# Expert rows through a transposing DMA on ScalarE's queue, with cleared slots and an early read of the overflow count

## The chip, the cores and the metric

The kernel runs on one core of one Trainium2 chip. A core has five engines that run their own instruction queues: TensorE (PE in the profile, its weight loads PEld), VectorE (DVE), ScalarE (ACT), GpSimd (POOL) and SyncE (SP). Sixteen DMA engines move data between HBM and the core's SBUF for all queues. The metric is device time in microseconds of one execution; less is better.

## What is computed

An attention without softmax, then a mixture of experts in which each token goes to one expert.

```python
kv = np.einsum('bhsd,bhse->bhde', k, v)          # 8 batches, 8 heads, 576 tokens, 64 wide
out = np.einsum('bhsd,bhde->bhse', q, kv)
rms = np.sqrt(np.mean(out * out, axis=-1, keepdims=True) + 1e-06)
x = out / rms * g_norm                            # as rows: N = 4608, D = 512
logits = x @ w_gate                               # E = 8 experts
expert_idx = np.argmax(logits, axis=1)
probs = softmax(logits); gate_w = probs[range(N), expert_idx]
for e in range(E):
    mask = expert_idx == e
    ye = np.maximum(x[mask] @ w1[e], 0.0) @ w2[e] # F = 1024
    out[mask] = gate_w[mask, None] * ye
```

## The kernel before

**Attention.** The outer loop (line 789) runs over the batches, with one more round for the last tiles. For batch b it forms the 64x64 products of k and v (`kv_mm`), transposes q (`t_mm`), folds the product with an identity and with the gate's weights (`fold_mm`), and copies the results out of PSUM (`x_copy`). Mixed into that, the output tiles of the batch before are made: `o_mm` on TensorE, the square on ScalarE and its sum on VectorE (`o_red`), the root by Ln and Exp (`o_nrm`), and the scaled row as fp16 with the gate's partial sums (`o_x`). Two batches make a pair j with nine tiles of 128 tokens. SyncE loads k, v and q for batch b+2 while b is worked on; a half batch is five loads.

**Rows.** A row of `xrow` holds 512 fp16 values, the gate's weight (fp32) and the token's number (int32): 516 words of 16 bits, `ROW`, 1032 bytes. One `xrow` buffer holds three tiles; there are four of them. `g_norm` is not in the rows.

**Routing.** When a chunk of tiles is done, `route` (line 685) runs in steps between the tiles: the expert by a maximum on VectorE, ranks by matmuls with a triangular matrix (`rps`), the row's slot in `posi`, and then one indirect DMA for each tile, issued by GpSimd (line 743), that scatters 128 rows into the DRAM tensor `x_slots`, where expert e owns N rows from e·N. The chunks of pairs 0 and 1 are whole, pair 2 is cut in (0,3) and (3,9), pair 3 in three. `jobs` is a queue; `job()` runs one step of its first entry, twice in each tile.

**Groups.** Experts 0 to 2 first take the rows of the first 384 slots that have been filled when pair 2 has been routed (`early_rows`, `EARLY_TILES` = 3), and later their slots 384 to 639. Experts 3 to 7 take 640 slots (`SLOT_TILES` = 5) at once. So `groups` are three of K=3 tiles, three of K=2 and five of K=5. What doesn't fit in 640 slots goes by tiles of 128: one spill tile is always computed ahead of the last group, others in a loop at the end (`For_i`, line 854) whose count `n_more` is read into registers of all engines (line 850).

**A group.** `fetch` gathers its rows by one indirect DMA a tile on GpSimd (line 291) into one of three buffers `xl`; slots that hold no row are skipped by an index out of bounds, so `xl` is zeroed at the start (line 788). `xpose` turns a tile by four TensorE transposes into PSUM `xps` (line 325), and VectorE copies it out, times `g_norm`, into `xsT` (line 328). `stage1` makes the eight blocks `hp` of the hidden layer (line 345), and ScalarE writes the relu `hT` (line 353). `stage2` makes a tile of output `yp` (line 361), VectorE multiplies it by the gate's weight (line 366), and GpSimd scatters it to the output by the tokens' numbers (line 369). Next group's `xpose` stands between the tiles of `stage2`. Group n+2 is fetched in stage 1 of group n.

**Weights.** Every `w_step` casts one staged block of weights from fp32 to fp16 on VectorE (line 220) and lets SyncE load another block of 0.52 MB (lines 206, 210); four blocks are in flight. Eight blocks make an expert.

**What sets the order.** The kernel is written under a manual schedule: each engine executes its instructions in the order in which the Python code issues them, and a tile framework puts in the semaphore waits. `ffn` is a generator; `unit()` advances it by one step, in the last round of the attention twice a tile from its fourth tile on (line 832). The loop at the end and line 850 stand behind the manual part.

Of the kernel before, what the change touches and what calls it, by code (L numbers as in the profile page):

```python
# [11 lines left out]
F32 = mybir.dt.float32  # L12
# [33 lines left out]
def kernel(  # L46
# [109 lines left out]
    for j in range(4):  # L156
# [7 lines left out]
    xl_ring = [  # L164
        P_const.tile([128, SLOT_TILES, ROW], I16, tag=f"xl{n}", name=f"xl{n}") for n in range(3)
    ]
# [13 lines left out]
    def w_load(pool, bufs):  # L180
# [34 lines left out]
        w_staged.append((e, dst, st))  # L215

    def w_cast(engine):
        if w_staged:
            e, dst, st = w_staged.pop(0)
            engine.tensor_copy(dst, st)  # L220
            w_done[e] = w_done.get(e, 0) + 1
# [4 lines left out]
    def w_step():  # L226
# [11 lines left out]
    srow = P_const.tile([128, 8, SLOT_TILES], F32, tag="srow")  # L238
    nc.vector.tensor_tensor(
        srow, _bc(cv["srank"], 1, 8), _bc(cv["ebase"], 2, SLOT_TILES), op=ALU.add  # L240
    )

    def row_index(name, ctr, ne, nk):
        bad = P_const.tile([128, ne, nk], F32, tag="bad" + name, name="bad" + name)
        nc.vector.tensor_tensor(
            bad, _bc(cv["srank"][:, 0:nk], 1, ne), _bc(ctr[:, 0:ne], 2, nk), op=ALU.is_ge
        )
        idx = P_const.tile([128, ne, nk], I32, tag="idx" + name, name="idx" + name)
        nc.vector.scalar_tensor_tensor(
            out=idx, in0=bad, scalar=BIG, in1=srow[:, 0:ne, 0:nk], op0=ALU.mult, op1=ALU.add  # L250
        )
        badi = P_const.tile([128, ne, nk], I32, tag="badi" + name, name="badi" + name)
        nc.vector.tensor_scalar(badi, bad, BIG, None, op0=ALU.mult)
        return idx, badi
# [3 lines left out]
    def early_rows():  # L258
# [6 lines left out]
        for i in range(EARLY):  # L265
            groups[i].fetch()
# [6 lines left out]
    class Group:  # L273
        def __init__(self, n, e, k0, k1):
# [4 lines left out]
            self.xl = xl_ring[n % 3]  # L279
# [8 lines left out]
        def fetch(self):  # L288
            idx = rows[self.table][0]
            for k in range(self.K):  # L290
                nc.gpsimd.indirect_dma_start(  # L291
                    out=self.xl[:, k, :], out_offset=None, in_=xs.ap(),
                    in_offset=IndirectOffsetOnAxis(
                        ap=idx[:, self.e, self.k0 + k : self.k0 + k + 1], axis=0
                    ),
                    bounds_check=E * N - 1, oob_is_err=False,
                )

        def slot_ids(self):
            badi = rows[self.table][1]  # L300
# [3 lines left out]
                self.xl[:, 0 : self.K, D + 2 : D + 4].bitcast(I32),  # L304
                badi[:, self.e, self.k0 : self.k0 + self.K].unsqueeze(2), op=ALU.max,
            )

# [6 lines left out]
        def start(self):  # L314
            self.xsT = self.pool().tile(
                [128, 4, self.n], F16, tag="xsT" + self.tag(), bufs=1, name="xsT"
            )

        def tag(self):
            return ""  # L320

        def xpose(self, k):
            ps = PSA.tile([128, 4, 128], F16, tag="KV", bufs=2, name="xps")
            for c in range(4):
                nc.tensor.transpose(  # L325
                    ps[:, c, :], self.xl[:, k, c * 128 : (c + 1) * 128].bitcast(F16), ident16
                )
            nc.vector.tensor_scalar(  # L328
                self.xsT[:, :, k * 128 : (k + 1) * 128], ps, g2, None, op0=ALU.mult
            )  # L330

        def stage1(self, f):
            if f == 0:
                self.hT = self.pool().tile(
                    [128, 8, self.n], F16, tag="hT" + self.tag(), bufs=1, name="hT"
                )
# [18 lines left out]
        def stage2(self, k):  # L355
            if self.small:
                yp = PSA.tile([128, D], F32, tag="O", bufs=2, name="yp")
            else:
                yp = PSA.tile([128, D], F32, tag="T", bufs=2, name="yp")
            for f in range(8):  # L360
# [6 lines left out]
                y, yp, self.xl[:, k, D : D + 2].bitcast(F32), None, op0=ALU.mult  # L367
# [10 lines left out]
    class SpillGroup(Group):  # L378
        def __init__(self, tables, col, view):
            self.tables, self.col, self.view = tables, col, view  # L380
            self.e, self.K, self.n, self.step, self.small = "s", 1, 128, 128, False

        def tag(self):
            return "d"
# [25 lines left out]

    class LoopGroup(SpillGroup):
# [3 lines left out]
        def fetch(self):  # L415
            super().fetch()
            self.wd = (
# [73 lines left out]
    tabs = []  # L491
# [4 lines left out]
    def ffn():  # L496
        order = list(groups)
        cur = order[0]
        cur.start()
        for k in range(cur.K):  # L500
            cur.xpose(k)
            yield
        n = 0
        while n < len(order):
# [4 lines left out]
            for f in range(8):  # L509
# [3 lines left out]
                if f == 0 and 1 <= real and EARLY <= real + 2 < len(groups):  # L513
                    groups[real + 2].fetch()
# [4 lines left out]
                if f == 3 and cur.e == EARLY + 1:  # L519
                    spill = SpillGroup(tabs[0], slice(0, 1), out_views[E * SLOT_TILES])  # L520
                    spill.fetch()
                    order.insert(len(order) - 1, spill)
                yield
            nxt = order[n + 1] if n + 1 < len(order) else None
            todo = []
            if nxt is not None:
                nxt.start()
                todo = list(range(nxt.K))
                nxt.xpose(todo.pop(0))
            for k in range(cur.K):  # L530
# [3 lines left out]
                while todo and len(todo) > max(cur.K - 2 - k, 0):  # L534
                    nxt.xpose(todo.pop(0))
# [13 lines left out]
    with tc.tile_pool(name="pattn", bufs=1) as PA:  # L549
# [55 lines left out]
        def fold_mm(b):  # L605
            folds[b] = [
                PSA.tile([128, 4, 72], F32, tag="T", bufs=2, name=f"fold{b}{y}")
# [12 lines left out]
        def x_copy(b):  # L620
            kvx[b] = PA.tile([128, 2, 4, 72], F32, tag="kvx", bufs=3, name=f"kvx{b}")
            nc.scalar.copy(kvx[b][:, 0], folds[b][0])
            nc.vector.tensor_copy(kvx[b][:, 1], folds[b][1])
# [269 lines left out]
```

## Time and profile before

Three runs took 325.21, 326.92 and 331.18 us; the median is 326.92. The profiled execution took 330.94 us.

| What | Before |
|---|---|
| time of the profiled execution | 330.94 us |
| span from first to last instruction | 329.2 us |
| mean granted TensorE clock | 0.903 |
| busy TensorE, share of the span | 269.0 us, 82% |
| busy VectorE | 183.4 us, 56% |
| busy ScalarE | 119.9 us, 36% |
| busy GpSimd | 137.6 us, 42% |
| moved by DMA | 85.79 MB, mean 261 GB/s |
| scatters into `x_slots` on GpSimd | 36, mean 991 ns |
| gathers of `xl` on GpSimd | 40, 32.4 + 9.9 us |
| transposes `xps` on TensorE | 164 matmuls, median 219 ns |
| copies into `xsT` on VectorE | 41, mean 477 ns |
| output scatters on GpSimd | 41, median 4.9 us from issue to landing |

A line of a timeline has the start, the duration, the engine, the line of the kernel, the operation, what it writes and reads, and in brackets how long the engine stood idle before and what ended that. A line of the waits names the waiting engine and line, what it waited for, the sum, the number of times and the longest. A line of the table by stretches has the stretch, its length, the busy time of each engine with its count, the granted clock, the busy share of the DMA engines and their rate.

### The profile page before, as it was taken

To read this page: it belongs to the slowest core of one execution; us is meant where nothing else is said; L and a number is where in the kernel's file an instruction comes from. 1 tells how busy PE (TensorE), PEld (TensorE's weight loads), DVE (VectorE), ACT (ScalarE), POOL (GpSimd) and SP (SyncE) were. 2 spreads that over 40 slices of the span, in tenths; PEclk is the share of its full clock that TensorE was granted. 3 is DMA by queue.
4 is the path that set the end of the run, shared out by engine and by line. 5 is a ranking of instruction groups with operands and counts; after the bars stand their busy time and mean duration, and the time that the engine had idled before them with its cause. 6 is when DMAs were issued, how large, how long until landed. Compare 5 with 4: busy or idle time off the path is not lost.

```text
span 329.2 us, 7247 instructions
## 1 busy us (share of the span) xinstructions
PE 269.0 (82%) x2759; PEld 189.3 (58%) x2759; DVE 183.4 (56%) x433; ACT 119.9 (36%) x316; POOL 137.6 (42%) x147
## 2 busy tenths in 40 slices
PE   0699897689766977564979996989999999997980
PEld 0587776577656866462535563657565665645630
DVE  6205566346745368889184678344657658375040
ACT  1136564436543445322322431326142240602600
POOL 9100001720076004384675462777477656052041
PEclk9999997959995589555999998999999999999996
DMA  6999999997897016799589894667799999983021
GB/s 158 334 368 367 369 368 367 381 282 216 246 323 295 18 67 167 250 323 324 201 260 372 295 322 121 214 214 251 250 339 358 351 397 279 408 284 130 0 99 55
DMA packets 45395, 85.79 MB, mean 261 GB/s; under 512 B 6188, under 2 KB 22829, under 8 KB 45360
## 3 DMA queue, kind: packets, MB, share of 16 engines
q1 hardware_dynamic: 36736, 66.07, 59.9%
q0 software_dynamic: 6976, 18.96, 15.6%
q10 hardware_dynamic: 1648, 0.29, 0.5%
q8 instruction: 22, 0.36, 0.4%
q14 instruction: 13, 0.11, 0.1%
HBM read 71.77 MB, written 15.50 MB: 265 GB/s over the span
## 4 chain that ended last, share of the span: by engine, by line
PE 26%; issue 11%; DMA 9%; POOL 7%; DVE 5%; POOLq 1%; ACT 0%; DVEq 0%; ACTq 0%
PE hp L345 13%; PE yp L361 11%; DMA out_dram<-y,d_id 7%; POOL out_dram L369 4%; POOL xl L291 2%; DMA xl<-x_slots,idxe 2%; PE xps L325 1%; DVE y L366 1%; DMA x_slots<-xrow,posi 1%; POOL x_slots L743 1%; DVE w1e L220 1%; DVE xsT L328 0%; POOLq L888 0%; POOLq L854 0%; DVE w2e L220 0%
## 5 line engine op out<-in xcount | busy, mean ns | idle before, releaser
L353 ACT ACTIVATE hT<-hp 128x320 f16<-128x320 f32 (+3 forms) x136 | 53.6, 426 | 106.5 <-PE hp L345 105.9
L345 PE MATMUL hp<-xsT,w1e 128*128 128x320 f16 (+2 forms) x512 | 76.6, 306 | 7.2 <-DVE xsT L328 6.3
L361 PE MATMUL yp<-w2e,hT 128*128 128x512 f16 x320 | 74.1, 379 | 0.3 <-DVE y L366 0.3
L369 POOL DMA_INDIRECT out_dram<-y,idv x40 | 44.6, 1115 | 60.3 <-DVE y L366 49.3
L345 PEld LDWEIGHTS <-w1e 128*128 128x128 f16 x512 | 51.0, 100 | 32.1 <-issue 11.7
L651 PE MATMUL ops<-kvx,qT 64*128 64x72 f32 (+1 forms) x640 | 48.0, 310 | 10.5 <-DVE lhat L680 9.6
L743 POOL DMA_INDIRECT x_slots<-xrow,posi x36 | 35.7, 991 | 40.5 <-DVE xrow L739 15.5
L651 PEld LDWEIGHTS ops<-kvx,qT 64*128 64x128 f32 (+1 forms) x640 | 42.3, 215 | 15.0 <-issue 9.3
L361 PEld LDWEIGHTS <-hT 128*128 128x128 f16 x328 | 30.8, 98 | 31.6 <-issue 0.4
L366 DVE TENSOR_SCALAR y<-yp,xl 128x512 f32<-128x512 f32 x40 | 30.0, 750 | 33.6 <-PE yp L361 29.9
L664 DVE TENSOR_REDUCE ms<-sq 128x8 f32<-128x512 f32 x36 | 24.6, 685 | 25.1 <-ACT sq L660 25.0
L291 POOL DMA_INDIRECT xl<-x_slots,idxa x31 | 32.4, 1046 | 11.7 <-issue 7.0
L594 PE MATMUL kvps<-mk,mv 128*64 128x64 f32 x640 | 28.7, 258 | 9.4 <-DMA mv<-in_v_dram 9.1
L676 DVE TENSOR_TENSOR xrow<-ops,rs 128x512 f16<-128x512 f32 x36 | 24.7, 686 | 18.0 <-DMA x_slots<-xrow,posi 9.3
L660 ACT ACTIVATE sq<-ops 128x512 f32<-128x512 f32 x36 | 21.5, 598 | 31.9 <-PE ops L651 31.5
L594 PEld LDWEIGHTS kvps<-mk,mv 128*64 128x64 f32 x640 | 26.0, 168 | 11.8 <-issue 10.3
L710 POOL COPY xrow<-tokc 128x3 int32<-128x3 int32 x12 | 3.0, 253 | 64.3 <-DVE xrow L676 64.2
L582 PE MATMUL tps<-ctile,mq 128*128 128x128 f32 x144 | 26.9, 320 | 3.5 <-ACT qT L583 1.9
L220 DVE CAST w2e<-wst 128x1024 f16<-128x1024 f32 x32 | 22.3, 704 | 11.4 <-DMA wst<-in_moe_w_dram 11.4
L583 ACT COPY qT<-tps 128x384 f32<-128x384 f32 x48 | 21.9, 473 | 14.4 <-PE tps L582 14.4
L328 DVE TENSOR_SCALAR xsT<-xps,g 128x512 f16<-128x512 f16 x41 | 19.2, 477 | 12.9 <-PE xps L325 12.7
L220 DVE CAST w1e<-wst 128x1024 f16<-128x1024 f32 x32 | 21.6, 688 | 4.5 <-DMA wst<-in_moe_w_dram 4.5
(99 smaller groups left out, 184.1 us busy)
## 6 DMA issues: line engine op xcount, KB each, us to landing
wst<-in_moe_w_dram SPq DMA_DIRECT2D x64, 512.0 KB, 5.8
mq<-in_q_dram SPq DMA_DIRECT2D x16, 576.0 KB, 7.8
mk<-in_k_dram SPq DMA_DIRECT2D x16, 320.0 KB, 7.5
mv<-in_v_dram SPq DMA_DIRECT2D x16, 320.0 KB, 7.3
mk<-in_k_dram SPq DMA_DIRECT2D x16, 256.0 KB, 7.9
mv<-in_v_dram SPq DMA_DIRECT2D x16, 256.0 KB, 7.1
wsts<-in_moe_w_dram SPq DMA_DIRECT2D x8, 512.0 KB, 5.9
out_dram<-y,idv POOLq DMA_INDIRECT x40, 4.9
```

Of the source, the lines that this page charges most:

```text
L220: engine.tensor_copy(dst, st)
L291: nc.gpsimd.indirect_dma_start(out=self.xl[:, k, :], out_offset=None, in_=xs.ap(), in_offset=IndirectOffsetOnAxis(ap=idx[:, self.e, self.k ...
L345: nc.tensor.matmul(hp, self.w()[0][:, kk, f * 128 : (f + 1) * 128], self.xsT[:, kk, s : s + self.step], start=(kk == 0), stop=(kk == 3),)
L353: nc.scalar.activation(self.hT[:, f, s : s + self.step], hp, ACTF.Relu)
L361: nc.tensor.matmul(yp, self.hT[:, f, k * 128 : (k + 1) * 128], self.w()[1][:, f, :], start=(f == 0), stop=(f == 7),)
L366: nc.vector.tensor_scalar(y, yp, self.xl[:, k, D : D + 2].bitcast(F32), None, op0=ALU.mult)
L369: nc.gpsimd.indirect_dma_start(out=self.views(k), out_offset=IndirectOffsetOnAxis(ap=self.ids[:, k : k + 1], axis=0), in_=y, in_offset=Non ...
L582: nc.tensor.transpose(ps[:, c, :], src[:, 128 * m : 128 * m + 128], cv["ident"])
L594: nc.tensor.matmul(kvps[b][64 * y : 64 * y + 64, 2 * u + a, :], main["v", b, u][:, 2 * y + a, c, :], main["k", b, u][:, 2 * y + a, c, :], ...
L651: nc.tensor.matmul(ps[p0 : p0 + 64 * n, y, o0 : o0 + 72], qT[b][hs, a, blk // 2 : blk // 2 + n, :].rearrange("d c p -> d (c p)"), kvx[b][h ...
L676: nc.vector.tensor_tensor(xr[:, 0:D].bitcast(F16).rearrange("p (a h d) -> p a h d", a=2, h=4), xv, _bc(rs2, 3, 64), op=ALU.mult,)
L743: nc.gpsimd.indirect_dma_start(out=xs_views[9 * j + t0 + t], out_offset=IndirectOffsetOnAxis(ap=posi[:, t : t + 1], axis=0), in_=xrow[j, ( ...
```

## The change

- The rows of a group come by two DMAs: one transposes 128·K rows of `x_slots` straight into `xsT` (two buffers), a small one loads the gate's weights and the tokens' numbers into `gi`. Groups 0 and 1 are fetched by SyncE, all later ones by ScalarE's queue, after the last relu of the group two before. The gathers, `xps` transposes and `xsT` copies of the groups are gone; the spill tile keeps them.
- `g_norm` is multiplied into `w1` when it is cast.
- As every slot is now read, the first 640 rows of each expert are cleared by DMA from a zeroed tile, two experts behind each of four half batches' loads; 640 rows are written as 128 runs of 5160 bytes.
- There are six `xrow` buffers instead of four, a further `yield` in `route` and two in `early_rows`, expert steps from the second tile of the last round on, and other PSUM tags for `fold` and the small groups' `yp`. The second half of `kvx` is copied by ScalarE.
- `n_more` is read in stage 1 of the second large group. The loop is inside the manual part, behind the last output scatter; the `fin` memset is gone.

```diff
-    xl_ring = [
-        P_const.tile([128, SLOT_TILES, ROW], I16, tag=f"xl{n}", name=f"xl{n}") for n in range(3)
-    ]
+    zrow = P_const.tile([128, SLOT_TILES * ROW], I16, tag="zrow")
+    nc.gpsimd.memset(zrow, 0)
+
+    def clear_slots(e):
+        nc.sync.dma_start(
+            xs.ap()[e * N : e * N + SLOTS].rearrange("(p k) w -> p (k w)", k=SLOT_TILES), zrow
+        )
...
     def w_cast(engine):
         if w_staged:
-            e, dst, st = w_staged.pop(0)
-            engine.tensor_copy(dst, st)
+            e, n, dst, st = w_staged.pop(0)
+            if n < 4:
+                engine.tensor_scalar(dst, st, g2, None, op0=ALU.mult)
+            else:
+                engine.tensor_copy(dst, st)
...
         yield
-        for i in range(EARLY):
-            groups[i].fetch()
+        yield
+        yield
+        for i in range(2):
+            groups[i].fetch(nc.sync)
         yield
...
-        def fetch(self):
-            idx = rows[self.table][0]
-            for k in range(self.K):
-                nc.gpsimd.indirect_dma_start(
-                    out=self.xl[:, k, :], out_offset=None, in_=xs.ap(),
-                    in_offset=IndirectOffsetOnAxis(
-                        ap=idx[:, self.e, self.k0 + k : self.k0 + k + 1], axis=0
-                    ),
-                    bounds_check=E * N - 1, oob_is_err=False,
-                )
+        def fetch(self, engine=nc.scalar):
+            r0 = self.e * N + 128 * self.k0
+            src = xs.ap()[r0 : r0 + self.n]
+            self.xsT = self.pool().tile([128, 4, self.n], F16, tag="xsT", bufs=2, name="xsT")
+            engine.dma_start(self.xsT, src[:, 0:D].bitcast(F16), transpose=True)
+            self.gi = P_fe.tile([128, SLOT_TILES, 4], I16, tag="gi", bufs=3, name="gi")
+            engine.dma_start(
+                self.gi[:, 0 : self.K], src[:, D:ROW].rearrange("(k p) w -> p k w", p=128)
+            )
...
-                if f == 0 and 1 <= real and EARLY <= real + 2 < len(groups):
-                    groups[real + 2].fetch()
                 if f == 5:
                     cur.slot_ids()
...
                     spill.fetch()
+                    n_more.append(
+                        nc.values_load(
+                            tabs[0][4][0:1, 0:1], min_val=0, max_val=MAXDYN - 1,
+                            skip_runtime_bounds_check_because="the count of tiles is bounded",
+                        )
+                    )
                     order.insert(len(order) - 1, spill)
+                if f == 7 and 0 <= real < len(groups) - 2:
+                    groups[real + 2].fetch()
                 yield
...
             kvx[b] = PA.tile([128, 2, 4, 72], F32, tag="kvx", bufs=3, name=f"kvx{b}")
             nc.scalar.copy(kvx[b][:, 0], folds[b][0])
-            nc.vector.tensor_copy(kvx[b][:, 1], folds[b][1])
+            nc.scalar.copy(kvx[b][:, 1], folds[b][1])
...
-                    [128, 3, ROW], I16, tag="xrow", bufs=4, name=f"xrow{j}{t}"
+                    [128, 3, ROW], I16, tag="xrow", bufs=6, name=f"xrow{j}{t}"
...
                             if b + 2 < B:
                                 load(b + 2, x // 3)
+                            if b in (1, 2):
+                                for e in range(2):
+                                    clear_slots(4 * (b - 1) + 2 * (x // 3) + e)
...
-                if b == B and n >= 3:
+                if b == B and n >= 1:
                     unit()
                     unit()
...
-    fin = P_const.tile([128, 1], F32, tag="fin")
-    nc.gpsimd.memset(fin, 0.0)
-    manual.close()
-
-    n_more = nc.values_load(
-        tabs[0][4][0:1, 0:1], min_val=0, max_val=MAXDYN - 1,
-        skip_runtime_bounds_check_because="the count of tiles is bounded by the tokens",
-    )
-    with tc.For_i(0, n_more) as it:
+    with tc.For_i(0, n_more[0]) as it:
         grp = LoopGroup(tabs[0], bass.ds(it + 1, 1), out_views[E * SLOT_TILES + 1])
...
+    manual.close()
```

## The prediction

> **What bounds the kernel now.** First the granted clock and span (329.2 us, mean clock 0.903), then the table by stretches, cut at the first `kvps` matmul of each batch of the attention and at the expert groups:
>
> ```profile
> core 0: us, PE busy (x) PEld busy (x) DVE busy (x) ACT busy (x) POOL busy (x), PEclk, DMA share, GB/s
> 33.00:45.80 12.80, 11.42 (x228) 9.86 (x226) 8.01 (x17) 8.10 (x23) 0.38 (x2) 1.00 1.07 369
> 60.60:79.20 18.60, 14.15 (x230) 12.36 (x228) 8.41 (x18) 8.42 (x23) 6.16 (x8) 0.82 0.96 306
> 92.60:116.20 23.60, 18.14 (x234) 15.39 (x232) 10.63 (x31) 9.06 (x24) 9.87 (x12) 0.61 0.55 202
> ```
>
> Batch 2 takes 12.8 us with the DMA engines full. Batches 4 and 6 do the same work in 18.6 and 23.6 us at clocks 0.82 and 0.61. The waits by line and TensorE's timeline say why:
>
> ```profile
> PE ops L651 <- DVE lhat L680: 9.6, 3, 3.9
> DVE xrow L676 <- DMA x_slots<-xrow,posi: 9.3, 2, 5.0
> ```
>
> ```profile
> 91.51 1.11 PE L651 MATMUL ops<-kvx,qT 64*128 64x72 f32 x16
> ...
> 101.26 1.98 PE L651 MATMUL ops<-kvx,qT 64*128 64x72 f32 x16 [3.21 <-DVE lhat L680]
> ```
>
> VectorE can't write `xrow` until an old scatter frees one of its four buffers; TensorE stands 3 to 4 us and then runs the same 16 matmuls in 1.98 instead of 1.11 us. Next comes GpSimd's timeline, where attention hands over to the experts:
>
> ```profile
> 133.98 0.96 POOL L743 DMA_INDIRECT x_slots<-xrow,posi  x1 [0.30 <-issue]
> 139.81 1.54 POOL L291 DMA_INDIRECT xl<-x_slots,idxe  x1 [4.87 <-DVE ms L664]
> ...
> 157.85 1.06 POOL L743 DMA_INDIRECT x_slots<-xrow,posi  x1 [5.14 <-issue]
> ```
>
> Nine gathers hold GpSimd for 12.6 us, and the next scatter waits until they have landed. This chain scatter, gather, scatter, not TensorE, sets the time from 127 to about 174. Then TensorE is the bound. In the large groups it is never idle, but the DMA engines are nearly full as well:
>
> ```profile
> 240.70:259.00 18.30, 18.30 (x125) 11.19 (x124) 11.89 (x24) 6.12 (x16) 13.16 (x13) 1.00 0.97 352
> 259.00:277.40 18.40, 18.40 (x126) 11.23 (x124) 11.63 (x20) 6.12 (x16) 11.42 (x11) 1.00 1.00 360
> ```
>
> **The skill.** "TensorE: Matmul & The Clock Gate", Part 1: The HAM clock gate, says that an idle window of about 3.4 us puts the array back to half rate; the 1.98 against 1.11 us agrees. "VectorE: DVE Perf Modes", Mode 2×_2P, says that a one-input scalar operation on f32 in SBUF runs at twice the basic rate, as a copy does; this trace has such casts (0.69 us for 1024 elements) but no multiply of that shape.
>
> **The change, part by part.**
>
> *Attention.* Six `xrow` buffers take the two scatter waits away. Batches 2, 3 and 5 last 12.8, 14.8 and 13.4 us, mean 13.7; if 4 and 6 become like them, 18.6+23.6−2×13.7 = 14.8 us are won. Against that:
> - Eight clears of 640 rows × 1032 B are 5.28 MB, at 367 GB/s 14.4 us of DMA time. They follow each half batch from 3u0 on. Before, a load lands 7.8 us after its issue: that leaves 4 us before use at batch 3 (issued to 33.9, used 45.8), 8 us at 4 and 16 at 5 (issued to 54.9, used 79.2). Delays grow by 3.6 us per half batch, so batches 3 and 4 are covered; batch 5, wanted at about 74.3, is 1 or 2 us late.
> - The first scatter waits for all clears: 23 MB / 0.367 = 63 us, plus the start, 68 to 71 instead of 56.6. Its three scatters (1.27 us apart) land at about 81, and the first expert row tile of pair 2 wants the buffer at 78. I count 2.7 us lost, the load being late within the same wait.
> - The zero fill stands ahead of the first load on GpSimd (2.2 us by the like fill of `xl`); other waits at the start fall away. I take 0.6, bounds 0 and 2.2. The second copy of `kvx` goes to ScalarE, 8 × 0.45 us, which is 40 to 60% busy there: nothing, at worst 3.6.
>
> Batch 7 so starts at 116.2−14.8+2.7+0.6 = 104.7.
>
> *Handover.* In the built order one more yield puts each scatter half a tile (1.6 us) later. The last scatters before the early fetch came 11.1 us after batch 7's start, so 117.4; the sixth is issued at 123.8 and lands 5.7 us later (the median), 129.5. SyncE then issues two transposes and two small loads, with all later weight loads queued behind them. What a transpose costs, the trace doesn't show. Issue: a load of 128 runs holds SP 0.34 us, one of 256 runs 0.60, so 2 ns a run; 384 rows in four pieces are 1536 runs, 3.1 us as the upper end, 0.34 the lower. Transfer: "DMA: Bandwidth & Descriptors", Latency and other measured facts, gives 261 GB/s, which is 1.5 us for 0.39 MB plus landing. So group 0 starts at 133.5 (before: 153.1). In between TensorE has nothing for about 9 us, and its clock will fall.
>
> The next links in order: seven weight loads of 0.52 MB, held behind the transposes, need 11 us; VectorE's casts of them stand ahead of the next routing, so the second scatter chunk goes out at 150 and lands at 159. ScalarE's first transpose waits for that; behind it in ScalarE's queue are the last `ex` and all of group 1's relus. Issue and small load take 2.5 us: free at 161.5. Group 1's first stage is 5.5 us, to 167. Its transpose waits for the last scatters (out at 163.5, landed 172): free at 174.5. Group 2: 5.5+5.2, to 185.2. Groups 3 to 5 take 4.1+3.5 each: 208. There the tables (8 us on VectorE) no longer stand ahead of `xsT`. Before groups 5 and 6 a five-tile transpose (2560 runs × 2 = 5.2 us at most, small load 1.3) overruns a 3.5 us second stage by some 1.5 us each. The first large group starts at 211 instead of 222.1: 11 us won.
>
> *Large groups.* Before, from 222.1 to the last matmul at 320.0: 98 us. After: five times 8.69+5×1.73 = 86.7; spill 2.86+0.22+1.73 = 4.8; the count read on TensorE, ten waits of 51 ns plus 0.74 us (as at the end now) = 1.25. Sum 92.8; the 0.22 us of each `xps` on the path and the stall around the spill are gone: 5.2 won. The casts with `g2` I take at the copy's 0.69 us; at half that rate 36 × 0.4 us more, covered by VectorE's third of idle time. The small loads are 640 pieces of 8 bytes; queue q10's 1648 small packets take 0.5% of 16 engines, 16 ns each, so 0.6 us of all engines a group, inside the weights' lead of 9 us (below).
>
> *End.* Now 9.2 us pass from the last matmul: the fifth scatter is issued behind the loop's exit, at 325.2. After: y 0.8, issue 1.1, landing 2.8 (median of the end), exit 2.1, close 0.8: 7.5, so 1.7 won.
>
> Sum: 329.2−11−5.2−1.7 = 311.3 of span. The median of the runs is 326.92/329.2 = 0.993 of this span: **309**.
>
> **Rivals.**
> *The clears and the new chain eat the gain.* For: VectorE waits on landings in every link above. Against: 14.8 us of stalls are plainly there. If attention and handover give nothing and only 5.2+1.7 stay: 322.3, so 320.
> *Slow transposes, slower than before.* In the large groups the other transfers are 6.0 MB, 16.7 us at 360 GB/s, of a 17.3 us group. A transpose of x us of all 16 engines overruns by x−0.6 a group; the last weight is cast 9 us before it's used, so the loss is 5(x−0.6)−9. It equals the gain of 17.9 at x = 6. The quoted 261 GB/s makes x = 2.5 and hides it; as fast as the gathers, 369 GB/s, x is 1.8. But "VectorE: DVE Perf Modes", The three transpose paths, has 1309 ns for 128x128, and 20 of those in a row are 26 us. At x = 10: 311.3+38, so 347. I take 2.5, since 1309 ns of one alone holds its landing.
> *Transposes a little slow.* x = 4 costs 8 us: 317. Rows of 1032 B, cut in quarters, speak for some loss.
>
> **How the numbers follow.** Forecast (298 to 318) 0.50; a little slow (312 to 322) 0.14; gain eaten 0.18; slow 0.18. The measurement can tell about 2%: 320.4 and 333.5. Faster: 0.50, plus 0.11 of the third case and half of the second rival's 0.18: 0.70. Within: 0.12. Slower: 0.18, all from slow transposes. Range 296 to 332: it leaves out the slow case and little at the low end, where the clock stays full; the forecast's own is 298 to 318.
>
> **What would show it.** Right: no wait of `ops` on `lhat` over 3 us in batches 4 and 6, batch 7's `kvps` near 105, `hp` of group 0 near 133, a large group in 17.3 us. Wrong: `hT` waiting on ScalarE's queue or `hp` on `xsT` in the large groups, or casts late on weights while the transposes fill the DMA engines.

## The result and the profile after

The changed kernel takes **365.98 us** (363.4 to 373.9, 4 runs), the kernel before 326.84 beside it: a ratio of 1.120, 95% interval 1.112 to 1.128. Here and below a ratio and its interval compare only those runs of each kernel that stayed near its fastest, so it can differ from the ratio of the two medians. The forecast was 309, the range 296 to 332. The profiled execution took 363.4 us, with a span of 361.6 at a mean clock of 0.868.

Set against the steps of the prediction (times from the span's start, us):

| step | forecast | measured |
|---|---|---|
| batch 7's first `kvps` | 104.7 | 102.1 |
| first `hp` of group 0 | 133.5 | 134.3 |
| stage 1 of group 1 done | 167 | 169.8 |
| group 2 starts | 174.5 | 174.9 |
| group 2 ends | 185.2 | 190.9 |
| first large group | 211 | 230.7 |
| from there to the last matmul | 92.8 | 116.1 |
| last matmul to the end of the span | 7.5 | 14.8 |

Down to the start of group 2 the prediction holds within 3 us. The last three rows are off by 19.7, 23.3 and 7.3 us, together 50.3: all of the distance between 311.3 and 361.6. The table by stretches of the changed kernel, cut at the starts of the groups from group 3 on (the columns are those shown above; the last two are the busy share of the DMA engines and what they moved):

```profile
core 0: us, PE busy (x) PEld busy (x) DVE busy (x) ACT busy (x) POOL busy (x), PEclk, DMA share, GB/s
190.90:213.90 23.00, 15.94 (x105) 10.11 (x104) 14.40 (x43) 6.50 (x18) 6.63 (x6) 0.95 1.02 181
213.90:230.70 16.80, 8.31 (x40) 4.87 (x40) 3.52 (x5) 2.57 (x7) 2.22 (x2) 0.70 1.18 132
230.70:250.30 19.60, 19.57 (x105) 11.03 (x105) 6.30 (x10) 6.12 (x16) 3.87 (x4) 0.88 1.15 216
250.30:268.00 17.70, 17.43 (x105) 10.13 (x104) 10.17 (x19) 6.12 (x16) 7.95 (x8) 1.00 1.12 332
...
276.70:307.30 30.60, 13.52 (x42) 4.92 (x40) 9.32 (x14) 0.77 (x2) 4.05 (x4) 0.72 0.99 206
```

The DMA engines count as full throughout. In four of these stretches they move 132 to 216 GB/s, where large groups of the kernel before had 352 to 360; but the large group from 250.3 took 17.7 us at 332 GB/s: by the packet records no transpose ran in its first 12.8 us. TensorE is busy for half of the second and less than half of the last stretch. Of the page, the queue's line of ScalarE's DMAs, first in the kernel before, then in the changed one:

```profile
q10 hardware_dynamic: 1648, 0.29, 0.5%
```

```profile
q10 hardware_dynamic: 23840, 4.78, 16.4%
```

4.5 MB more take 16.4% of 361.6 us less 0.5% of 329.2, which is 57.7 us of all 16 engines. ScalarE's fetches hold 4352 rows (384, three times 256, five times 640), so 640 rows cost 8.5 us in the mean, their small loads included, where the forecast had 2.5. This is the time that packets took; they can overlap (the share passes 1), so it isn't time in which nothing else moves. By the packet records the five 640-row transposes took 9.6, 11.7, 6.1, 6.1 and 9.6 us. Who waits is in the timelines. ScalarE's:

```profile
202.96 9.52 ACTq L292 DMA_TRANSPOSE xsT<-x_slots  x1
212.59 0.82 ACTq L294 DMA_DIRECT2D gi<-x_slots  x1
213.52 0.66 ACT L337 ACTIVATE hT<-hp 128x256 f16<-128x256 f32 x2 [10.26 <-issue]
...
218.85 12.60 ACTq L292 DMA_TRANSPOSE xsT<-x_slots  x1
```

TensorE's:

```profile
213.95 4.86 PE L329 MATMUL hp<-xsT,w1e 128*128 128x256 f16 x24 [6.78 <-ACT hT L337]
...
230.73 11.08 PE L329 MATMUL hp<-xsT,w1e 128*128 128x320 f16 x64 [8.47 <-DMA xsT<-x_slots]
...
304.31 3.19 PE L345 MATMUL yp<-w2e,hT 128*128 128x512 f16 x8 [7.97 <-DVE y L350]
```

and VectorE's:

```profile
277.12 0.75 DVE L225 TENSOR_SCALAR w1e<-wst,g 128x1024 f16<-128x1024 f32 x1 [8.13 <-DMA wst<-in_moe_w_dram]
...
302.85 0.75 DVE L225 TENSOR_SCALAR w1es<-wsts,g 128x1024 f16<-128x1024 f32 x1 [9.87 <-DMA wsts<-in_moe_w_dram]
```

Issuing one 640-row transpose holds ScalarE's queue for 9.5 and 12.6 us. Behind the first of them ScalarE makes no relu for 10.3 us, and TensorE waits 6.8 us for it. The transposed rows of the first large group then land 8.5 us after TensorE is free. From 277 on it is the weights that come late: a cast stands ahead of the `y` that frees TensorE's next PSUM buffer, so `yp` waits with it (8.0 us at 304.31).

### The profile page after: what moved, and what is told of

The parts are those of the page before. It is cut to its first block, busy times and chain, and to the rows that moved or that the text cites. A ratio compares the mean times of both kernels' runs of the same rounds, so it can differ in the third digit from the quotient of the medians.

```text
span 361.6 us, 6790 instructions
## 1 busy us (share of the span) xinstructions
PE 264.8 (73%) x2599; PEld 176.5 (49%) x2599; DVE 159.3 (44%) x382; ACT 119.8 (33%) x324; POOL 92.0 (25%) x104
## 3 DMA queue, kind: packets, MB, share of 16 engines
q10 hardware_dynamic: 23840, 4.78, 16.4%
## 5 line engine op out<-in xcount | busy, mean ns | idle before, releaser
L329 PE MATMUL hp<-xsT,w1e 128*128 128x320 f16 (+2 forms) x512 | 84.8, 326 | 31.2 <-ACT hT L337 15.4
L345 PE MATMUL yp<-w2e,hT 128*128 128x512 f16 x320 | 77.3, 400 | 17.5 <-DVE y L350 17.5
L329 PEld LDWEIGHTS <-w1e 128*128 128x128 f16 x512 | 53.3, 105 | 61.2 <-issue 40.0
L345 PEld LDWEIGHTS <-hT 128*128 128x128 f16 x328 | 33.1, 101 | 58.5 <-issue 25.1
L350 DVE TENSOR_SCALAR y<-yp,gi 128x512 f32<-128x512 f32 x40 | 29.8, 749 | 61.3 <-PE yp L345 55.8
L734 POOL DMA_INDIRECT x_slots<-xrow,posi x36 | 36.8, 1021 | 67.4 <-DMA mk<-in_k_dram 26.3
L641 PE MATMUL ops<-kvx,qT 64*128 64x72 f32 (+1 forms) x640 | 44.1, 294 | 9.1 <-DVE lhat L670 9.1
L641 PEld LDWEIGHTS ops<-kvx,qT 64*128 64x128 f32 (+1 forms) x640 | 38.7, 200 | 15.4 <-DVE lhat L670 6.7
L584 PE MATMUL kvps<-mk,mv 128*64 128x64 f32 x640 | 28.6, 253 | 18.6 <-DMA mv<-in_v_dram 17.1
L225 DVE TENSOR_SCALAR w1e<-wst,g 128x1024 f16<-128x1024 f32 x32 | 23.7, 752 | 30.4 <-DMA wst<-in_moe_w_dram 29.5
L584 PEld LDWEIGHTS kvps<-mk,mv 128*64 128x64 f32 x640 | 25.7, 164 | 21.6 <-issue 16.6
L572 PE MATMUL tps<-ctile,mq 128*128 128x128 f32 x144 | 26.3, 314 | 2.9 <-DMA mq<-in_q_dram 1.2
L650 ACT ACTIVATE sq<-ops 128x512 f32<-128x512 f32 x36 | 21.6, 600 | 18.8 <-PE ops L641 18.6
L573 ACT COPY qT<-tps 128x384 f32<-128x384 f32 x48 | 22.1, 473 | 13.7 <-PE tps L572 13.5
L658 ACT ACTIVATE rs<-ms,epsb 128x8 f32<-128x8 f32 x36 | 10.8, 301 | 30.8 <-DVE ms L654 30.7
L572 PEld LDWEIGHTS tps<-ctile,mq 128*128 128x128 f32 x144 | 17.4, 157 | 7.3 <-ACT qT L573 2.9
```

The costliest lines, as they stand in the source:

```text
L225: engine.tensor_scalar(dst, st, g2, None, op0=ALU.mult)
L329: nc.tensor.matmul(hp, self.w()[0][:, kk, f * 128 : (f + 1) * 128], self.xsT[:, kk, s : s + self.step], start=(kk == 0), stop=(kk == 3),)
L345: nc.tensor.matmul(yp, self.hT[:, f, k * 128 : (k + 1) * 128], self.w()[1][:, f, :], start=(f == 0), stop=(f == 7),)
L350: nc.vector.tensor_scalar(y, yp, self.gate(k), None, op0=ALU.mult)
L572: nc.tensor.transpose(ps[:, c, :], src[:, 128 * m : 128 * m + 128], cv["ident"])
L584: nc.tensor.matmul(kvps[b][64 * y : 64 * y + 64, 2 * u + a, :], main["v", b, u][:, 2 * y + a, c, :], main["k", b, u][:, 2 * y + a, c, :], ...
```

## The experiments

The changed kernel's time scatters, from 341 to 374 us over its runs, and times differ with the chip. The kernel before took 327 to 330 us on the chips of the first runs and of sets 2 and 3, and 354 to 356 on those of sets 1, 4 and 5. Only ratios within a set are compared. Theory A: a transposing transfer that runs beside other queues' transfers holds the DMA engines far longer than alone. Rival B: the engines are well, and only ScalarE's held queue costs. Rival C: the clears, the casts with `g2` or the new chain cost it.

### Set 1: no transposes, one queue, transposes on TensorE, transfers alone

Rows loaded as they lie (this leaves out their turning; sizes and counts stay):

```
-            engine.dma_start(self.xsT, src[:, 0:D].bitcast(F16), transpose=True)
+            engine.dma_start(
+                self.xsT.rearrange("p c n -> p (c n)").rearrange("p (k d) -> p k d", d=D),
+                src[:, 0:D].bitcast(F16).rearrange("(k p) d -> p k d", p=128),
+            )
```

> The changed kernel, but the rows are loaded as they lie, in 1024-byte runs, into the same buffers by the same queues at the same places: the rows are not transposed, so the first matmuls of the experts work on the wrong layout; their sizes and number are the same. Theory A (transposing transfers that run beside weight loads hold the 16 DMA engines far longer than their bytes, and the weights come late): the 43 us lost between the first large group and the last matmul go; first large group near 211 instead of 230.7, 93 us of large groups instead of 116; with the end as it is, a span of 318 and a time near 320. Rival B (the queue of ScalarE is held while a transpose is issued, relus wait behind it): the plain issue is shorter too, so also 320 to 335. Rival C (clears, casts with g2, or the new chain of scatter and fetch cost the time): stays above 350.

Measured 334.58 us, 0.947 of the kernel before (0.938 to 0.957). From the first large group, at 225.5 and not near 211, to the last matmul 91.9 us.

All fetches on SyncE:

```
-        def fetch(self, engine=nc.scalar):
+        def fetch(self, engine=nc.sync):
```

> The changed kernel with all eleven fetches issued on SyncE, in the queue of the weight loads, none on ScalarE. Rival B (held ScalarE queue): hp's waits for the relus (15.4 us) go, about 346, and the DMA share stays where it was. Theory A in the form that two queues have to run side by side: transposes and weight loads now come one after the other in one queue, a 640-row transpose takes about 3.4 us of the engines, about 330. Theory A in the form that any traffic beside a transpose hurts: weights as late as before or later, 355 to 370.

Measured 345.21 us, 0.975 (0.960 to 0.990).

Whole rows loaded as they lie, and transposed on TensorE as before (part of the edit):

```
+            self.xl = self.pool().tile(
+                [128, EARLY_TILES if self.small else SLOT_TILES, ROW], I16, tag="xl", bufs=3, name="xl"
+            )
+            engine.dma_start(
+                self.xl[:, 0 : self.K, :],
+                xs.ap()[r0 : r0 + self.n].rearrange("(k p) w -> p k w", p=128),
+            )
```

> The changed kernel without the DMA transpose: ScalarE (SyncE for the first two) loads the whole rows of a group as they lie from the cleared slots, and TensorE transposes them as in the kernel before, with g_norm put in there; the casts are plain again. Clears, six xrow buffers, early count and the loop kept behind the last scatter stay. Theory A: group 0 starts near 135 as in the changed kernel, the first large group near 209, large groups 98 us as before, the end 14.8 as in the changed kernel: span 320, time 318 to 324. Rival C: above 345.

Measured 362.54 us, 1.020 (1.007 to 1.033). That was not what Theory A said. The edit had left the small groups' `yp` in the PSUM buffers of `xps`; set 4 puts it back.

Transfers alone:

> Only transfers, none of the computation, six stages one after the other: (1) four 640-row transposes on ScalarE's queue alone; (2) twelve 512 KB weight loads alone on SyncE's; (3) both at once from the two queues; (4) both from SyncE's queue in turn (three loads, one transpose); (5) as 3 with plain row loads in place of the transposes; (6) the four transposes beside eight 1 MB row stores on SyncE's queue. Theory A: stage 1 about 14 us (3.4 each), stage 2 about 17 to 20, stage 3 well over their sum, 45 or more, stage 5 about 25, stage 4 near the sum. Rival B: stage 3 no more than the sum of 1 and 2, with 1 short.

VectorE touches each buffer when its transpose has landed:

```profile
20.97 0.15 DVE L100 CAST acc<-x 128x1 f32<-128x1 f16 x1 [1.79 <-DMA x<-x_slots]
23.78 0.15 DVE L100 CAST acc<-x 128x1 f32<-128x1 f16 x1 [2.66 <-DMA x<-x_slots]
26.92 0.15 DVE L100 CAST acc<-x 128x1 f32<-128x1 f16 x1 [2.99 <-DMA x<-x_slots]
29.55 0.15 DVE L100 CAST acc<-x 128x1 f32<-128x1 f16 x1 [2.47 <-DMA x<-x_slots]
```

The four transposes alone landed 2.6 to 3.1 us apart, so 2.9 for 640 rows, and each issue held ScalarE's queue for 2.9 to 3.1 us. In stage 3 the buffers were set back so slowly that the two kinds hardly met: inconclusive for the mixing. No time of this set can be held against the first runs, since the kernel before took 355.5 here; the next set repeats what matters beside the changed kernel.

### Set 2: beside the changed kernel

> The changed kernel unchanged, for comparison with the others of this set on one chip: on the chip of the first set the kernel before took 355 us instead of 327, so only ratios within a set are read. All theories: 1.08 to 1.15 of the kernel before if that ratio doesn't depend on the chip.

Measured 351.75 us (340.6 to 370.7, 4 runs), the kernel before 328.57.

> The changed kernel with plain row loads in place of the transposes (rows not transposed, so the experts work on the wrong layout; all sizes and counts the same), beside the changed kernel on one chip. Theory A (transposes beside weight loads hold the DMA engines): 40 us less than the changed kernel, large groups of 17.4 us, weights on time. Rival B (only ScalarE's queue held at issue): 15 to 25 us less. Rival C (clears, casts, chain): within 5 us of the changed kernel.

Measured 315.49 us, 0.963 of the kernel before (0.954 to 0.972). That is 36 less than the changed kernel by the medians, and 25 less than its fastest run, so the time alone doesn't tell Theory A (40 less) from Rival B (15 to 25). Rival C falls: clears, casts and chain are all in it. The table by stretches, cut at its five large groups:

```profile
core 0: us, PE busy (x) PEld busy (x) DVE busy (x) ACT busy (x) POOL busy (x), PEclk, DMA share, GB/s
206.80:224.20 17.40, 17.40 (x106) 10.21 (x105) 8.97 (x14) 6.12 (x16) 6.18 (x6) 1.00 0.99 321
...
241.90:259.30 17.40, 17.40 (x106) 10.20 (x105) 9.91 (x15) 6.12 (x16) 6.28 (x6) 1.00 1.03 367
259.30:276.80 17.50, 17.50 (x109) 10.36 (x108) 10.18 (x16) 6.12 (x16) 6.42 (x6) 1.00 0.95 333
276.80:298.70 21.90, 21.48 (x145) 12.77 (x143) 6.54 (x11) 8.13 (x24) 6.23 (x7) 1.00 0.34 130
```

TensorE is busy nearly all the time, a large group takes the 17.4 us that the prediction summed, and while weights are loaded the same bytes from the same rows in the same queue leave the engines at 321 to 367 GB/s. This edit takes both away, though: the mixing, and the held queue.

The end undone:

```
+    fin = P_const.tile([128, 1], F32, tag="fin")
+    nc.gpsimd.memset(fin, 0.0)
+    manual.close()
+
     with tc.For_i(0, n_more[0]) as it:
```

> The changed kernel with only its end undone: the manual order is closed, after a small memset, ahead of the overflow loop, as in the kernel before; the early read of the count stays. In the changed kernel 14.8 us passed from the last matmul to the end of the span, in the kernel before 9.2. If the loop kept in the manual order costs that: last matmul to end 9 or less, 5 us faster than the changed kernel. If the early read or something else costs it: 14 to 15, no change.

Measured 357.3 us (344.0 to 369.0), and 16.6 us from the last matmul to the end: neither 9 nor 14.8. The last scatter goes out 8.2 us after the last matmul, behind the loop's exit, so keeping the loop behind it does win 1.8 us of the end, as forecast (1.7). The lengthening of the end is elsewhere.

Transfers alone again, now meeting:

> Transfers alone, none of the computation, in stages: (1) four 640-row transposes on ScalarE's queue; (2) twelve 512 KB weight loads on SyncE's; (3) both begun together; (4) plain row loads in place of the transposes, begun together with the weights; (5) transposes and weights in turn in SyncE's queue; (6) transposes with six 1 MB stores on SyncE's queue; (7) as 3 with three 1 MB stores on GpSimd's queue as well. The earlier transfer kernel hardly overlapped the two kinds; alone a 640-row transpose took 2.8 us there. Theory A: (3) well over the sum of (1) and (2), 40 us or more against 11+19; (4) about 25; (5) about the sum. If transposes and weight loads simply share the engines: (3) 30 or less.

One run. The table by stretches, one row for each of stages 2 to 6 (weights alone; two queues; plain rows; one queue; with stores):

```profile
core 0: us, DVE busy (x) POOL busy (x), PEclk, DMA share, GB/s
32.40:51.10 18.70, 2.12 (x26) 0.00 (x0) 1.00 0.86 337
51.20:92.50 41.30, 2.58 (x34) 0.00 (x0) 1.00 1.09 216
92.60:118.90 26.30, 2.32 (x31) 0.00 (x0) 1.00 0.92 339
119.00:149.20 30.20, 2.48 (x34) 0.00 (x0) 1.00 1.01 295
149.30:183.90 34.60, 0.72 (x18) 0.00 (x0) 1.00 1.05 258
```

Four transposes alone are 11.4 us (4 × 2.86, from m1), the twelve weight loads alone took 18.7: sum 30.1. In one queue they take 30.2. From two queues, with no engine computing but for VectorE's touches, they take 41.3, though the DMA share says that the engines are full. The same rows as plain loads beside the same weights take 26.3. That is Theory A: the transposes are slow here though ScalarE has nothing else to do. One of their issues held its queue for 17.7 us, so the long hold in the kernel, too, comes with the mixing. Stage 6 mixes with stores: its first transpose landed only 22 us after the stage began, so it isn't weight loads alone. Stage 7 adds stores to stage 3 and took 47.6 us. Stage 1 was run into by the clears of its own preparation and isn't used.

### Set 3: one queue beside the changed kernel, and the end

> The changed kernel unchanged, to stand beside the others of this set on one chip. 340 to 371 where the kernel before takes 328 (the second set), 364 to 366 beside 327 (the first runs): it varies from run to run, which Theory A explains by how transposes and weight loads happen to meet.

Measured 360.63 us (346.4 to 368.3), the kernel before 329.78.

> The changed kernel with all fetches issued on SyncE, so that transposes and weight loads go through one queue, one after the other. The transfer kernel took 30.2 us for four transposes and twelve weight loads in one queue, 41.3 from two. Theory A: 18 us or more under the changed kernel, large groups under 18.5 us each, run to run within 2%. Rival B (ScalarE's held queue alone): the same gain would come with relus no longer waiting, but the DMA engines' rate in the large groups would stay near 210 GB/s; Theory A has it above 290.

Measured 329.2 us (325.2 to 334.8, 20 runs). That is 31 less than the changed kernel by the medians, 17 less than its fastest run, and 1.010 of the kernel before (1.003 to 1.017). The runs lie 2.9% apart, not within 2%. Its large groups in the table by stretches (this execution took 333.3 us, 4 above the median):

```profile
core 0: us, PE busy (x) PEld busy (x) DVE busy (x) ACT busy (x) POOL busy (x), PEclk, DMA share, GB/s
212.20:229.60 17.40, 17.35 (x105) 10.18 (x105) 8.65 (x14) 6.12 (x16) 5.12 (x5) 1.00 1.15 294
229.60:247.40 17.80, 17.49 (x106) 10.17 (x105) 10.27 (x19) 6.12 (x16) 8.24 (x8) 1.00 1.04 343
247.40:268.00 20.60, 17.55 (x106) 10.15 (x105) 9.16 (x14) 6.12 (x16) 5.39 (x5) 1.00 1.06 293
268.00:294.80 26.80, 20.29 (x110) 10.96 (x109) 10.87 (x17) 6.12 (x16) 6.23 (x6) 0.87 1.00 306
```

The engines move 293 to 343 GB/s (Rival B had near 210), the first large group starts at 212.2, where the prediction had 211, and the first two take their 17.4 and 17.8 us. Then the weights are late after all, so "under 18.5 each" was missed: 104.5 us to the last matmul instead of 92.8. At 2.9 us a transpose, on top of 16.7 us of other transfers, would be 2.2 more than a 17.4 us group has room for, 11 us in five groups. That is an estimate: by the packet records the five transposes took 3.5 to 6.3 us here, so one queue doesn't bring back the time alone. The waits of `hp` on `hT` fall from 15.4 to 3.8 us and those on `xsT` from 15.2 to 6.8: taking the issue off ScalarE is part of the gain, and this edit can't part it from the rest.

The same with the count read late and the loop outside:

```
+    n_more = nc.values_load(
+        tabs[0][4][0:1, 0:1], min_val=0, max_val=MAXDYN - 1,
+        ...
+    )
```

> As the kernel with all fetches on SyncE, and the end as in the kernel before: the count is read after the last group, the manual order is closed ahead of the loop. From the last matmul to the end: 9.2 us if the early read (or what goes with it) costs the 5.6 us, else 14 to 16. In all 5 us faster than the same kernel with the early read.

Measured 329.6 us, 1.009 (1.004 to 1.013), end 16.6 us: no gain, and no 9.2.

The kernel before with only the early read:

> The kernel before with one edit: the overflow count is read in the fifth group (fourth step), as in the changed kernel, instead of after the last group; the loop stays where it was, after the manual order is closed. If the early read makes GpSimd's closing work long: end 13 to 16 us after the last matmul instead of 9.2, 4 to 6 us slower than before. If not: 8 to 9, the same time.

Measured 330.23 us, end 9.1 us: no change. So neither the early read nor the loop's place makes the end long. The raw trace has, at the end of the changed kernel and of those made from it so far, a drain instruction of GpSimd of 6.44 us after everything has landed (7.75 where the loop stands outside; the views leave such instructions out); in the kernel before the drain lasts 3.35 us and its last scatter lands within it.

### Set 4: row loads mended, and the number of GpSimd's DMAs

`yp` of the small groups back in its own PSUM buffers (what differs from the row loads of set 1):

```
-                yp = PSA.tile([128, D], F32, tag="KV", bufs=2, name="yp")
+                yp = PSA.tile([128, D], F32, tag="O", bufs=2, name="yp")
```

> The changed kernel without the DMA transpose: whole rows of the cleared slots loaded as they lie on ScalarE's queue, turned on TensorE as in the kernel before, small groups' yp back in the PSUM buffers of the kernel before, so that xps and yp no longer share two. Theory A: group 0 near 135, the first large group near 205, large groups 98 us, end 14.5: span 317, 0.96 to 0.975 of the kernel before. If the row loads beside the weights cost as the transposes did: 1.0 or more.

Measured 356.29 us, 1.001 (0.996 to 1.006) on a chip where the kernel before takes 356.27. First large group 241.0, then 98.8 us, then 14.3. By its time it lies where the expectation put row loads that cost as much as the transposes. By the stretches it doesn't: the large groups and the end are as expected, but group 0 starts at 161.0 and not near 135, and the first large group comes 80.0 us later (72.9 with the plain rows of set 1). The attention is slow on this kind of chip (below), so its gain could not be seen here.

The same with GpSimd's gathers:

> As the kernel with row loads, but the rows come by GpSimd's indirect gathers, one for each 128 rows, as in the kernel before (all 640 slots are gathered, since the free ones are cleared). If the number of GpSimd's DMAs sets the end: 9 us from the last matmul, else 14.5. The handover is then again scatter, gather, scatter on GpSimd: first large group 6 to 10 us later than with row loads; together within 1% of the kernel with row loads.

Measured 357.2 us, 0.995 (0.987 to 1.003); end 8.5 us.

Row loads, with forty small transfers that nothing uses:

```
+            for k in range(self.K):
+                i = len(small_dmas)
+                small_dmas.append(nc.gpsimd.dma_start(idle[:, i : i + 1], c_tok.ap()[:, 0, 0:1]))
```

> As the kernel with row loads, with forty added transfers of 128 x 4 bytes issued by GpSimd, one for each row tile fetched, that nothing uses. If the number of GpSimd's DMAs sets the end: 9 to 10 us from the last matmul instead of 14.5. If not the number, but the gathers as such: 14.5.

Measured 355.92 us (one run); end 7.7 us instead of 14.3. But its last matmul ends at 346.0, without the forty transfers at 339.8: the whole got no shorter. GpSimd issues 118 DMAs in this kernel, in that with gathers and in the kernel before, and 78 in the changed kernel.

### Set 5: forty idle transfers at the start

All three kernels of this set have:

```
+        idle = P_const.tile([128, 40], I32, tag="idle", name="idle")
+        for i in range(40):
+            nc.gpsimd.dma_start(idle[:, i : i + 1], c_tok.ap()[:, 0, 0:1])
         load(0, 0)
```

> The changed kernel with forty transfers of 128 x 4 bytes that nothing uses, issued by GpSimd at the start of the attention, where it is idle for some 25 us. If the count of GpSimd's DMAs over the program sets the end: 8 us from the last matmul instead of 14.8. If only what GpSimd did lately counts: 14.8. The rest as in the changed kernel, 335 to 365.

Measured 374.78 us (365.2 to 387.1), above the 335 to 365 expected, the kernel before 354.05; end 8.8 us, with the forty transfers over 330 us earlier. So it is the count over the program, or what follows from it, and not what GpSimd did last. The ends of the changed kernel's and of this kernel's timelines (all engines), each beside its span:

```profile
core 0 of [0], span 361.6 us
...
346.84 0.75 DVE L350 TENSOR_SCALAR y<-yp,gi 128x512 f32<-128x512 f32 x1 [0.98 <-PE yp L345]
347.86 0.98 POOL L353 DMA_INDIRECT out_dram<-y,idv  x1 [0.74 <-POOLq L838]
```

```profile
core 0 of [0], span 375.4 us
...
366.67 0.75 DVE L350 TENSOR_SCALAR y<-yp,gi 128x512 f32<-128x512 f32 x1 [0.98 <-PE yp L345]
367.70 0.98 POOL L353 DMA_INDIRECT out_dram<-y,idv  x1 [0.58 <-issue]
```

After the same last scatter 13.7 us pass in the one and 7.7 in the other.

> The kernel with all fetches on SyncE's queue and the same forty transfers at the start. Without them 1.01 of the kernel before. If the count sets the end: 6.7 us less, 0.985 to 0.995 of the kernel before; else 1.01.

Measured 346.32 us, **0.984** (0.976 to 0.992); end 8.9. One queue for transposes and weights with a short end is a little faster than the kernel before on this chip, by less than the 2% that can be told safely. What the short end is worth in time isn't shown: the same kernel without the forty transfers had 0.975 (0.960 to 0.990) in set 1, on a chip of the same kind. On a chip of the faster kind, from 1.010 of 329.8 less 6 us, it would be near 0.99; that is an estimate, not run.

> The kernel with row loads on ScalarE's queue, turned on TensorE, and the same forty transfers at the start. Without them 1.00 of the kernel before on a chip where that takes 356 us. If the count sets the end: 0.98; on a chip where the kernel before takes 328 us the attention's gain should show more, 0.955 to 0.975.

Measured 352.64 us, 0.998 (0.993 to 1.002), not 0.98; end 8.0. Row loads turned on TensorE are no faster than the kernel before where that takes 354 us.

## Why the prediction was wrong, step by step

**Attention.** Right in its sum, in part by luck. Batch 6 lasts 13.7 us (before 23.6), as the removed scatter wait said. Batch 4 lasts 18.1 (before 18.6), and its gain did not come: its `kvps` wait 1.9 and 1.6 us for `mv`, whose loads stand in one queue with the clears, and the clock is 0.73. The prediction had batch 4 covered and batch 5 late. The 4.4 us lost are more than the 2.7 set down; batches 3 and 5 were shorter in return (13.9 and 12.1 us for 14.8 and 13.4). Batch 7 came 2.6 us earlier than forecast. The first scatter went out at 73.7 instead of 68 to 71.

**Handover.** Right: group 0 at 134.3 for 133.5, and the two transposes on SyncE, in a quiet stretch, issued in 1.6 and 1.4 us. Group 2 then lost 3.7 us because its relus stood behind the next transpose, which waited for the last scatters.

**Groups 3 to 5.** Wrong: 25.8 us were forecast from the end of group 2 to the first large group, 39.8 measured. The step is the five-tile transpose at "5.2 us at most", overrunning by 1.5 us each. The bound came from a load's 2 ns a run, with the queue empty (and by its own terms, 5.2 and 1.3 against 3.5, it allows 3.0). Measured were 5.3 to 12.6 us for 640 rows when weights were under way, against 2.9 to 3.1 alone in the transfer kernel, and 1.2 to 1.6 for 256 and 384 rows earlier. The long hold comes with the traffic beside it, and no row of the profile before could show it.

**Large groups.** The step that failed is "the quoted 261 GB/s makes x = 2.5 and hides it". Alone, x is 2.9 (229 GB/s), so the number was near, and the 1309 ns a tile of the rival don't add up. What was wrong is to add it: the sum took transfers of different queues to share the engines without loss. Mixed with weights from another queue a 640-row transpose cost 5.7 us in the transfer kernel ((41.3−18.7)/4; its packets alone say 5.7 too) and 8.5 in the changed kernel, beyond the 6 from which the rival said "slower". (The 369 GB/s that the prediction gave to gathers is the rate of batch 2's loads; no gather runs there.) The rival's own formula, 5(x−0.6)−9, gives 30.5 us for 8.5; 43.0 were lost by the last matmul, since it prices only the large groups, and the late rows and held relus ahead of them come on top. The rest of the sum stands: with plain rows the large groups take 91.9 us for the 92.8 forecast, and the whole kernel 315.5.

**The lead of 9 us** of the weights was taken as a reserve. Whether it is one stays open. In one queue the large groups lost 11.7 us. At 2.9 us a transpose the five overruns of 2.2 us would make that without any reserve; at the 5.1 us that the packets took in the mean, 5(5.1−0.6)−9 = 13.5 makes it with the reserve spent. Both are estimates.

**End.** The order of scatter and loop won its 1.8 us. The term forgotten is GpSimd's drain: with 40 of its 118 DMAs gone the end grew by 5.7 us (14.8 for 9.1). That the whole kernel gains as much when the end is short again, no run shows.

**The chances.** The mechanism that happened was the second rival, given 0.18, at 347; the range ended at 332 and left it out. With a cost bounded by 1.8 and 26 us and a break-even at 6, the range had to reach to it.

What stays open: what in the engines makes mixed transposes slow, the turning itself or their 256-byte packets (plain rows have 1024-byte ones; plain rows in 256-byte pieces were not run); how the loss divides between slow transfers and ScalarE's held queue; why GpSimd's drain depends on the number of its DMAs; and why the same kernel takes 327 us on some chips and 355 on others, so that row loads with TensorE's transposes were not measured where the attention is fast. The traces show where chips part: with plain rows (sets 2 and 1) batch 5 starts at 73.2 and 73.4, group 0 at 130.9 and 152.6. In between, from 74 to 160, TensorE stands 0.2 and 13.4 us where the profile names nothing it waits for. Every trace of a whole kernel agrees: at most 0.2 us in sets 2 and 3 and the first runs, 8.9 to 16.5 in sets 1, 4 and 5.

## What to carry to other kernels

Price a transfer of a new kind beside the traffic that it will meet and not alone, and see which queue it comes from: here transposes and weights took 30 us in one queue and 41 from two. Where a queue belongs to an engine that also computes, look at what stands behind the issue: here ScalarE made no relu for 10.3 us. And when DMAs of one engine are taken away, look at the end of the program as well as at the work that they did.

## What the runs showed of the hardware

- A transposing DMA of 640 rows of 1024 bytes: 2.9 us alone, 5.7 us (transfer kernel) and 8.5 in the mean (changed kernel) beside weight loads from another queue. These slow down with it: their packets took 229 ns in the mean there, 186 in one queue, 166 alone. The DMA share doesn't tell the cases apart: 1.03 for the transposes alone (at 207 GB/s), 1.09 from two queues (216), 1.01 in one (295). In the packet records of the changed kernel the transposes' 256-byte packets on ScalarE's queue take 18 ns at the median and 49.5 in the mean; those of SyncE's two transposes in the quiet handover 21.7 in the mean.
- The end of the program after GpSimd's last scatter: 13.7 us with 78 DMAs issued by GpSimd, 7.7 with 118 (the changed kernel with the forty transfers), through a drain of 6.44 against 1.06 us.
- A cast with a per-partition multiplier takes 0.75 us for 1024 f32 elements, a plain one 0.69.
